# One kernel, four small moves in a hand-written order: a score copy ahead of a sign, and the first sorting for expert slots taken in one go

## The chip, the core and the metric

The kernel runs on one core of a Trainium2 chip. The metric is the device time of one execution in microseconds, as a median over runs. A core has five engines that run beside each other: TensorE (PE in the profile; its weight loads are PEld), VectorE (DVE), ScalarE (ACT), GpSimd (POOL) and SyncE (SP, which only issues transfers here). Each engine takes its own instructions strictly in the order in which the program gives them, and waits for the others through semaphores. So where an instruction stands in its engine's row is part of the program.

## What is computed

Attention with 8 batches, 8 heads, 576 positions and 64 features a head, in which every query keeps only its 32 largest scores; its output, as 4608 rows of 512, then goes through a layer of 8 experts of which each row takes one.

```python
scores = scale * np.matmul(q, k.transpose(0, 1, 3, 2))
kth = np.partition(scores, -32, axis=-1)[..., -32:-31]
scores = np.where(scores >= kth, scores, -1e9)
attn = np.exp(scores - scores.max(-1, keepdims=True))
attn = attn / (attn.sum(-1, keepdims=True) + 1e-09)
x = (attn @ v).transpose(0, 2, 1, 3).reshape(4608, 512)

logits = x @ w_gate
e_idx = np.argmax(logits, axis=1)
gate_w = softmax(logits)[np.arange(4608), e_idx]
eom = 1.0 / (1.0 + np.exp(-(x @ w_output_gate)))
for e in range(8):
    m = e_idx == e
    h = np.maximum(x[m] @ w1[e], 0.0)
    out[m] = gate_w[m, None] * eom[m, e, None] * (h @ w2[e])
```

## The kernel before

**Steps.** The queries are cut into 36 tiles of 128 rows, and each tile into four pairs of heads: 144 steps. Step i works on several pairs at once. On DVE it ranks the candidates of pair i (L317, L320), then for pair i-1 it does `spot` (L370, a small TENSOR_TENSOR), two window maxima (L359), the group maxima of pair i+1 (L309, 16 of them), then `pick` (L376, a small TENSOR_TENSOR), the threshold (L382) and the weighing of the exponentials by the threshold (L397). On ACT it makes two signs (L344) that POOL turns into the windows (L347, two TENSOR_TENSOR of 128x576), exponentials (L354), and copies out of PSUM. On PE it transposes the weighed exponentials of pair i-2 (L424), multiplies those of pairs i-4 and i-3 by the values in every second step (L456), and makes scores of a later pair (L282).

**Calm steps.** The first 40 steps (`LONE` = 40) are called calm in the code. In them the odd head of each pair is not weighed on DVE: DVE only negates its threshold (`less`, L385), ACT takes a sign with it (L404), POOL adds scores and sign (L407, a TENSOR_TENSOR of 128x576), and one step later ACT takes the exponential (L413). L404 and L407 are made by `veil`, for pair i-1 in step i; L413 by `unveil`, for pair i-2. Scores are made two pairs ahead there: PE's matmuls (L282) come after the last single transpose, which needs L413, and ACT's copy of them into SBUF (L290) is the first entry of a list `last` that runs after `veil`. In calm steps with an odd number PE also makes 24 (or 12) transposes that nobody reads (L977).

**Experts.** Every finished tile gets gate logits. After the tiles named in `SORTS` their rows are sorted (`group_route`, some 17 small DVE operations and two on ACT, with one matmul product between), and each tile's 128 list entries are scattered to DRAM by a GpSimd transfer (L589). `slot_picks` then chooses which experts get slots of 128 rows now, and how many; `queue_slots` puts them in `order`. In all 31 slots are made during the attention and 9 after it. The small operations wait in queues (`urgent`, `small`), of which `fill(n)` emits n at fixed places of a step; transfers wait in `slow`, from which `run_slow` emits as many as fit a budget (`DMAS` = 2.6, 2.0 in calm steps).

**A slot.** SP loads the slot's list of rows (L757), 2 MB of `w1` (L742) and 2 MB of `w2` (L749); GpSimd gathers its rows of x (L765); PE turns them (L775); then four pieces follow, one a step: two up (L786, 16 matmuls in the program, shown as 32 rows in the profile, each followed by a Relu on ACT, L794) and two down (L801). `ahead` fetches; `heavy_start` and `heavy_piece` set the pieces on PE's row. In the program before, the first slot is queued in step 38 and its first piece is in step 42, and from then on there is a piece in each step: 27 slots begin within the 144 steps and the four that drain the pipeline. A short stretch follows in which pieces already begun are finished, one with each call of `background`; there the last route, the table of the last slots and a check (`unsettled`, whose one matmul is L185) are made. The other 13 slots are worked after it in another form (L1107), with 48 matmuls of 512 columns each.

Of the kernel before, what the change touches and what calls it, by code (L numbers as in the profile page):

```python
# [23 lines left out]
P = 128  # L24


SORTS = ((4, 0), (7, 5), (11, 2), (13, 3), (16, 3), (19, 4), (23, 4), (27, 3), (30, 3), (32, 4))

USUAL = 9

# [2 lines left out]
DMAS = 2.6  # L33
# [5 lines left out]
def tile_topk_attention_moe(  # L39
# [39 lines left out]
    ids = dram.tile([NID, 4], I32, name="ids")  # L79
# [3 lines left out]
    for bp in range(NB // 2):  # L83
        for j in range(9):
# [4 lines left out]
            else:  # L89
                TT.append(((2 * bp + 1, j - 5),))  # L90
    sorts = [x for x in SORTS if x[0] < NTT]
    ENDS, EARLY = zip(*sorts) if sorts else ((), ())
    assert all(n <= E for n in EARLY) and E == 8
    ends = list(ENDS) + [NTT]
    GROUPS = [list(range(a, b)) for a, b in zip([0] + ends, ends)]
# [96 lines left out]
    def run(exact, stack):  # L192
# [15 lines left out]
        small = deque()  # L208
# [14 lines left out]
        def run_slow(budget, kinds):  # L223

            for x in [x for x in slow if x[2] in kinds]:
                if spent[0] + x[3] > budget:
                    return
                slow.remove(x)
                spent[0] += x[3]
                x[4]()  # L230

        def flush(what):
            for x in [x for x in slow if x[2] == what]:
                slow.remove(x)
                spent[0] += x[3]
                x[4]()

        def waiting(what):
            return any(x[2] == what for x in slow)

        def fill(n=1):
            for _ in range(n):
                if urgent:
                    urgent.popleft()()
                elif small and small[0]() is not False:
                    small.popleft()
# [64 lines left out]
        def rank(i, r):  # L311
            if exact:
                return
            vs, cs = VV[i]
            cs = [c.rearrange("p (g k) -> p g k", k=8)[:, :, :REACH[r]] for c in cs]
            for a in range(2):
                nc.vector.max(out=vs[:, a, 8 * r:8 * r + 8], in_=cs[a])  # L317
            if r < 2:
                for a in range(2):
                    nc.vector.match_replace(out=cs[a], in_to_replace=vs[:, a, 8 * r:8 * r + 8],  # L320
                                            in_values=cs[a], imm_value=LOW)
# [501 lines left out]
        NSTEP = NTT * NHP  # L823
# [3 lines left out]
        order = []  # L827
# [5 lines left out]
        def ahead(what, f, n, after=None, lag=0):  # L833

            while had[what] < min(len(order), cur[0] + n):
                s = had[what]
                if after and when.get((after, s), clock[0]) + lag > clock[0]:
                    return
                f(s, *order[s])
                when[what, s] = clock[0]  # L840
                had[what] += 1

        def queue_slots(g, n, rows):
            flush("x")
            assert rows_done[0] >= rows
            order.extend((g, k, rows) for k in range(n))
            known[0] = step[0] + (0 if had["id"] == cur[0] and not heavy else 1)
# [3 lines left out]
        def ids_known():  # L851

            ahead("id", fetch_id, len(order))
            assert had["id"] - cur[0] <= NLIST - 2
# [6 lines left out]
        def ahead_of_slot():  # L861

            clock[0] += 1
            fetch_ahead()
# [32 lines left out]
        def side_use():  # L897
            if uses:
                fill(len(urgent))
                uses.pop()()  # L900
# [22 lines left out]
            nc.tensor.transpose(awake[:, 0, :], ident, ident)  # L923
        scores(0)(((0, 1), (1, 2)))

        def route(g):
            small.extend(group_route(g, LGT[g]))
            if g < NGRP - 1 and EARLY[g]:
                small.extend(slot_picks(g))
                small.append(lambda: not waiting("ids"))  # L930
                small.append(lambda: queue_slots(g, EARLY[g], (GROUPS[g][-1] + 1) * P))
                small.append(lambda: step[0] >= known[0] and ids_known())
# [6 lines left out]
        for i in range(NSTEP + 4):  # L939
            t, hp = divmod(i, NHP)  # L940
            step[0] = i
            if i + 1 < NSTEP and (i + 1, 0) not in SC:
                scores(i + 1)()


            calm = i < LONE and not exact
            for r in range(3):
                if i < NSTEP:
                    rank(i, r)
                    if r == 0:  # L950
                        shift(i)
                if not calm:
                    fill(1)
            spent[0] = 0.0
            run_slow(SUMS, ("x",))
            spent[0] = 0.0
            if i < NSTEP:
                below(i)
            early, late, last = [], [], []
            mid, beside = None, None  # L960
            if calm and 2 <= i:
                first_copy = flip(i - 2, 0)
                mid = ps_t.tile([P, 4, P], F32, name="pst")
                f = side_start()
                beside = f(mid) if f else None
                first_copy()
            if 2 <= i < NSTEP + 2:
                unveil(i - 2)
            if calm:
                exps(i)  # L970
            if 4 <= i < NSTEP + 4 and i % 2 == 0:
                early.append(attend(i - 4))
            elif 2 <= i < LONE:

                idle = ps_m.tile([P, 4, P], F32, name="pm")
                for c in range(12 if beside else 24):
                    nc.tensor.transpose(idle[:, c % 4, :], ident, ident)  # L977
            if mid is not None:
                early.append(flip(i - 2, 1, beside, mid))
            elif 2 <= i < NSTEP + 2:  # L980
                early.append(flip(i - 2, 0))
                early.append(flip(i - 2, 1, side_start()))
            if calm and i + 2 < NSTEP:
                last.append(scores(i + 2))
            if i >= NSTEP + 2:
                extra = side_start()
                if extra:
                    early.append(extra(ps_t.tile([P, 4, P], F32, name="pst")))

            room = not uses  # L990
            ahead_of_slot()
            heavy_start()
            ev = heavy_piece()
            if ev:
                late.append(ev)
            if 2 <= i < NSTEP + 2:
                (last if calm else late).append(flip(i - 2, 2))
            ev = turn_ahead() if room or not heavy else None
            if ev:
                (last if calm else late).append(ev)  # L1000
            for f in early:
                f()
            if i < NSTEP and not calm:
                exps(i)
            for f in late:
                f()
            if 1 <= i <= NSTEP:
                spot(i - 1)
                window(i - 1, 0)
                window(i - 1, 1)  # L1010
            if i + 1 < NSTEP:
                gmax(i + 1, 0)
            if i + 1 < NSTEP:
                gmax(i + 1, 1)
            if 1 <= i <= NSTEP:
                pick(i - 1)
            if not calm:
                fill(1)
            if 1 <= i <= NSTEP:
                choose(i - 1)  # L1020
                fill(5 if calm else 1)
                weigh(i - 1)
            ahead("x", fetch_x, 2, "id", 1)
            run_slow(DMAS - 0.6 if calm else DMAS, ("ids", "out"))
            if 1 <= i <= NSTEP:
                veil(i - 1)
            for f in last:
                f()
            side_use()
            fill(3)  # L1030
            if i < NSTEP:
                if hp == 0 and t + 2 < NTT:
                    load_q(t + 2)
                if i == 0:
                    small.extend(([] if exact else setup()) + [clear_ids])
                jj = t % 9
                b2 = t // 9 * 2
                for j0, b in ((0, b2 + 1), (5, b2 + 2)):
                    n = (jj - j0) * NHP + hp
                    if b < NB:  # L1040
                        if n == 1:
                            load_k(b)
                        if n == 6:
                            load_v(b)
            if i >= 3 and (i - 3) % NHP == NHP - 1:
                tt = (i - 3) // NHP
                if tt == GROUPS[gi][0]:
                    LGT[gi] = st.tile([P, max(map(len, GROUPS)), 16], F32, name="lg", bufs=2)
                tile_rows(tt, gi, LGT[gi], tt - GROUPS[gi][0])
                if tt == GROUPS[gi][-1]:  # L1050
                    gi += 1
# [263 lines left out]
```

## Time and profile before

| | |
|---|---|
| median of 3 runs | 1270.94 us (1270.91 to 1271.02) |
| the profiled execution's own time | 1270.56 us |
| its span in the trace | 1268.8 us, so 1.76 us lie around it |
| mean granted TensorE clock | 0.984 |
| PE, DVE busy | 1178.6 and 1178.5 us |
| ACT, POOL busy | 1021.7 and 692.0 us |

How to read it: the trace gives every instruction a line of the code, a start, and what its engine waited for. A row of the timeline is start, duration, engine, line, operation, output and inputs, number merged; in brackets the idle time ahead of it and who ended it. A row of windows gives, for a stretch of the span, the busy time of PE, PEld, DVE, ACT and POOL with instruction counts, then the granted PE clock (1.00 is full speed), the share of the transfer engines and GB/s.

### The profile page before, as it was taken

To read this page: it belongs to the slowest core of one execution; us is meant where nothing else is said; L and a number is where in the kernel's file an instruction comes from. 1 tells how busy PE (TensorE), PEld (TensorE's weight loads), DVE (VectorE), ACT (ScalarE), POOL (GpSimd) and SP (SyncE) were. 2 spreads that over 40 slices of the span, in tenths; PEclk is the share of its full clock that TensorE was granted. 3 is DMA by queue.
4 is the path that set the end of the run, shared out by engine and by line. 5 is a ranking of instruction groups with operands and counts; after the bars stand their busy time and mean duration, and the time that the engine had idled before them with its cause. 6 is when DMAs were issued, how large, how long until landed. Compare 5 with 4: busy or idle time off the path is not lost.

```text
span 1268.8 us, 30920 instructions
## 1 busy us (share of the span) xinstructions
PE 1178.6 (93%) x9769; PEld 894.7 (71%) x9769; DVE 1178.5 (93%) x6045; ACT 1021.7 (81%) x1958; POOL 692.0 (55%) x1048
## 2 busy tenths in 40 slices
PE   6887778879999999999999999999999999899996
PEld 5665555557777777777777777777777777678885
DVE  7999999999999999999999999999999994689984
ACT  6999999987888778878888888878888884388883
POOL 6666676674467665664564475456556663232110
PEclk8999999988999999999999999999999999899998
DMA  5400210237446555656557556554444445899981
GB/s 138 78 18 18 72 56 18 56 118 245 167 165 204 174 203 179 215 192 222 183 197 228 189 184 204 182 202 167 167 167 167 167 165 213 317 376 396 391 310 60
DMA packets 109376, 227.39 MB, mean 179 GB/s; under 512 B 14855, under 2 KB 33543, under 8 KB 108177
## 3 DMA queue, kind: packets, MB, share of 16 engines
q1 hardware_dynamic: 99824, 205.67, 47.0%
q0 software_dynamic: 7552, 18.96, 4.2%
q8 instruction: 79, 1.29, 0.4%
q10 hardware_dynamic: 1824, 0.67, 0.3%
q14 instruction: 97, 0.79, 0.2%
HBM read 206.68 MB, written 20.69 MB: 179 GB/s over the span
## 4 chain that ended last, share of the span: by engine, by line
DVE 66%; PE 15%; issue 11%; ACT 5%; POOL 1%; DMA 1%; DVEq 0%; POOLq 0%; SPq 0%; ACTq 0%
DVE cand L309 20%; DVE v L359 12%; DVE ep L397 11%; DVE cand L320 7%; DVE v L317 6%; PE pm L786 4%; PE po L456 3%; DVE x L376 2%; PE ps L282 2%; DVE x L370 2%; DVE kth L382 2%; PE pst L424 1%; PE pm L801 1%; PE pm L1107 1%; ACT marks L344 1%
## 5 line engine op out<-in xcount | busy, mean ns | idle before, releaser
L347 POOL TENSOR_TENSOR w<-s,marks 128x576 f32<-128x576 f32 x288 | 363.3, 1283 | 202.6 <-ACT marks L344 183.1
L309 DVE MAX8 cand<-s 128x8 f32<-128x72 f32 x2304 | 321.9, 216 | 12.9 <-ACT s L290 12.8
L424 PE MATMUL pst<-ident,ep 128*128 128x128 f32 x1296 | 206.3, 283 | 46.0 <-ACT ep L413 32.5
L344 ACT ACTIVATE marks<-s,v 128x576 int8<-128x576 f32 x288 | 220.6, 770 | 23.8 <-DVE v L317 21.7
L432 ACT ACTIVATE pT<-pst 128x512 f32<-128x512 f32 (+1 forms) x432 | 197.7, 483 | 51.8 <-PE pst L424 50.4
L424 PEld LDWEIGHTS pst<-ident,ep 128*128 128x128 f32 x1296 | 145.5, 141 | 132.9 <-issue 48.7
L786 PE MATMUL pm<-xs,w1t 128*128 128x128 f32 x1792 | 212.3, 277 | 0.0
L786 PEld LDWEIGHTS pm<-xs,w1t 128*128 128x128 f32 x1792 | 206.7, 194 | 0.2 <-issue 0.2
L359 DVE MAX8 v<-w 128x8 f32<-128x576 f32 x288 | 203.3, 746 | 0.0
L397 DVE SCALAR_TENSOR_TENSOR ep<-s,kth,ep 128x576 f32<-128x576 f32 x248 | 194.8, 817 | 8.6 <-DVE kth L382 0.5
L290 ACT ACTIVATE s<-ps 128x1152 f32<-128x1152 f32 (+1 forms) x145 | 162.2, 1120 | 50.3 <-PE ps L282 49.9
L801 PE MATMUL pm<-w2t,ht 128*128 128x512 f32 x432 | 194.4, 593 | 0.0
L456 PE MATMUL po<-pT,v 128*64 128x128 f32 (+3 forms) x3200 | 186.4, 268 | 0.0
L282 PE MATMUL ps<-kst,qst 64*128 64x288 f32 (+1 forms) x1280 | 179.5, 428 | 5.2 <-ACT s L290 5.2
L354 ACT ACTIVATE ep<-s,v 128x576 f32<-128x576 f32 x248 | 181.0, 779 | 3.1 <-POOL v L333 3.1
L456 PEld LDWEIGHTS po<-pT,v 128*64 128x64 f32 (+1 forms) x3200 | 159.0, 137 | 33.7 <-issue 31.9
L812 POOL DMA_INDIRECT out_dram<-y,idt x40 | 45.6, 1140 | 160.5 <-ACT y L808 147.8
L801 PEld LDWEIGHTS pm<-w2t,ht 128*128 128x128 f32 x432 | 78.0, 191 | 77.5 <-issue 77.5
L317 DVE MAX8 v<-cand 128x8 f32<-128x24 f32 (+2 forms) x864 | 132.2, 194 | 0.0
L282 PEld LDWEIGHTS ps<-kst,qst 64*128 64x128 f32 (+1 forms) x1280 | 97.0, 176 | 44.2 <-issue 17.5
L320 DVE MATCH_REPLACE8 cand<-v,cand 128x24 f32<-128x24 f32 (+1 forms) x576 | 97.5, 178 | 0.0
L333 POOL TENSOR_SCALAR v<-v 128x2 f32<-128x2 f32 x144 | 32.8, 227 | 113.8 <-DVE v L317 112.7
(185 smaller groups left out, 1689.6 us busy)
## 6 DMA issues: line engine op xcount, KB each, us to landing
w1t<-in_w_dram SPq DMA_DIRECT2D x40, 2048.0 KB
w2t<-in_w_dram SPq DMA_DIRECT2D x40, 2048.0 KB
v<-in_va_dram SPq DMA_DIRECT2D x8, 1152.0 KB
x_rows<-xu SPq DMA_DIRECT2D x36, 256.0 KB
qst<-in_qa_dram SPq DMA_DIRECT2D x70, 128.0 KB
kst<-in_ka_dram SPq DMA_DIRECT2D x14, 576.0 KB
ids<-far SPq DMA_DIRECT2D x1, 678.0 KB
xg<-x_rows,idt POOLq DMA_INDIRECT x40, 6.4
```

The costliest lines, as they stand in the source:

```text
L282: nc.tensor.matmul(ps[qs, a, n, :288], Q[t][rows, hp, qs], K[b][rows, hp, cols], start=True, stop=True)
L309: nc.vector.max(out=c[:, 8 * g:8 * g + 8], in_=SC[i, a][:, g * GW:(g + 1) * GW])
L317: nc.vector.max(out=vs[:, a, 8 * r:8 * r + 8], in_=cs[a])
L344: nc.scalar.activation(m.bitcast(I8).rearrange("p (s b) -> p s b", b=2)[:, :, 1], s, AF.Sign, bias=vs[:, a, PIVOT - 1:PIVOT], scale=-(1.0 ...
L347: nc.gpsimd.tensor_tensor(w, s, m, op=ALU.add)
L359: nc.vector.max(out=VV[i][0][:, a, 24:32], in_=SW[i][0][a])
L397: nc.vector.scalar_tensor_tensor(e, SC.pop((i, a)), kth_col(i, a), e, op0=ALU.is_ge, op1=ALU.mult, accum_out=SM[t][:, 2 * hp + a:2 * hp + ...
L424: nc.tensor.transpose(ps[:, c - c0, :], pt[:, c * P:(c + 1) * P], ident)
L432: nc.scalar.activation(x, ps[:, :n, :], AF.Copy)
L456: nc.tensor.matmul(po[a * 64:(a + 1) * 64, k, qs], lhs, rhs, start=half and not k and not m, stop=(c == 3 and k == 1 and m == len(TT[t]) - 1))
L786: nc.tensor.matmul(ph[:, f - f0, :], w[:, c, f * P:(f + 1) * P], XS[s][:, c, :], start=(c == 0), stop=(c == NC - 1))
L801: nc.tensor.matmul(PY[s], HT[s][:, f, :], w[:, f, :], start=(f == 0), stop=(f == NF - 1))
```

## The change

Four edits. In calm steps the copy of the scores (L290), first in the list `last`, is put ahead of `veil`'s sign of the odd head (L404). The first sorting covers five tiles instead of four; it has no slots (`(5, 0)`), so the second sorting, the first with slots, covers tiles 5 and 6 instead of 4 to 6. From the second route on until its slots are queued a flag `hurry` holds: `fill(60)` takes all small operations that can go, at two places of the step, with the open use of PE's side product (`side_use`) ahead of the first; the budget of `run_slow` is 3.4. And the first slots are queued, listed and get their first `w1` and `w2` fetched in the same step (`first_fetches`).

```diff
-SORTS = ((4, 0), (7, 5), (11, 2), (13, 3), (16, 3), (19, 4), (23, 4), (27, 3), (30, 3), (32, 4))
+SORTS = ((5, 0), (7, 5), (11, 2), (13, 3), (16, 3), (19, 4), (23, 4), (27, 3), (30, 3), (32, 4))
...
+        hurry = [False]
+
+        def first_fetches():
+            hurry[0] = False
+            ids_known()
+            ahead("w1", fetch_w1, 1)
+            ahead("w2", fetch_w2, 1)
+
         def route(g):
             small.extend(group_route(g, LGT[g]))
             if g < NGRP - 1 and EARLY[g]:
                 small.extend(slot_picks(g))
+                if not order:
+                    hurry[0] = True
+                    small.append(lambda: not waiting("ids"))
+                    small.append(lambda: queue_slots(g, EARLY[g], (GROUPS[g][-1] + 1) * P))
+                    small.append(first_fetches)
+                    return
...
             if 1 <= i <= NSTEP:
                 choose(i - 1)
-                fill(5 if calm else 1)
+                if hurry[0]:
+                    side_use()
+                fill(60 if hurry[0] else 5 if calm else 1)
                 weigh(i - 1)
             ahead("x", fetch_x, 2, "id", 1)
-            run_slow(DMAS - 0.6 if calm else DMAS, ("ids", "out"))
+            run_slow(DMAS + 0.8 if hurry[0] else DMAS - 0.6 if calm else DMAS, ("ids", "out"))
+            if last and calm and i + 2 < NSTEP:
+                last.pop(0)()
             if 1 <= i <= NSTEP:
                 veil(i - 1)
             for f in last:
                 f()
             side_use()
             fill(3)
+            if hurry[0]:
+                fill(60)
```

In the order of instructions the first edit shows on ACT in every calm step. This is the place in step 2, rows with a minus from the program before, with a plus from the changed one; `marks_81` is the sign of the odd head, `s` the copied scores, `pT` copies of transposes, `marks_79` the first sign of the next step:

```order
 L354 ACTIVATE ep<-s,v_286 128x576
 L432 ACTIVATE pT_385<-pst 128x128
-L404 ACTIVATE marks_81<-s,less 128x576
-L290 ACTIVATE s<-ps 128x1152
+L290 ACTIVATE s<-ps 128x1152
+L404 ACTIVATE marks_81<-s,less 128x576
 L432 ACTIVATE pT_397<-pst 128x512
 L344 ACTIVATE marks_79,n<-s,v_403 128x576
```

Only L404 and L290 have changed places; all else on ACT stays as it was in these steps.

The other edits move the experts' pieces. This is PE's row in step 37, a calm step, in the program before: transposes, the idle ones (L977), one transpose more, the scores, and the transposes of the end of this step and the start of the next.

```order
L424 MATMUL pst<-ident,ep 128x128 x8
L977 MATMUL pm<-ident 128x128 x24
L424 MATMUL pst<-ident,ep 128x128
L282 MATMUL ps<-kst,qst 128x288 x4
L424 MATMUL pst<-ident,ep 128x128 x8
```

And the same step in the changed program, where L991 is the line of the idle transposes:

```order
L424 MATMUL pst<-ident,ep 128x128 x4
L991 MATMUL pm<-ident 128x128 x24
L424 MATMUL pst<-ident,ep 128x128
L282 MATMUL ps<-kst,qst 128x288 x4
L786 MATMUL pm<-xs,w1t 128x128 x16
L424 MATMUL pst<-ident,ep 128x128 x4
L775 MATMUL pst<-ident,xg_124 128x128 x4
L424 MATMUL pst<-ident,ep 128x128 x4
```

The first piece of the first slot (L786) has come into step 37, behind the scores, and with it the turn of the second slot's rows (L775); the idle transposes stay. In the changed program pieces stand in steps 37 to 56 and from 59 on; 28 slots begin ahead of the tail instead of 27, and 12 are left for the last form instead of 13.

At the end of the attention this stands on PE around L185, the matmul of the check, before (L558 is the last product of the route; L1086 turns rows for the last form):

```order
L558 MATMUL pst<-oh_17003,ones_b 128x8
L801 MATMUL pm<-w2t,ht 128x512 x4
L185 MATMUL po<-lo,ones 1x2
L786 MATMUL pm<-xs,w1t 128x128 x16
L1086 MATMUL pm<-ident,xg_124 128x128 x4
```

And in the changed program:

```order
L558 MATMUL pst<-oh_17038,ones_b 128x8
L801 MATMUL pm<-w2t,ht 128x512 x4
L775 MATMUL pst<-ident,xg_124 128x128 x4
L801 MATMUL pm<-w2t,ht 128x512 x4
L185 MATMUL po<-lo,ones 1x2
L786 MATMUL pm<-xs,w1t 128x128 x16
```

One down piece more stands between the route's product and the check's matmul.

## The prediction

> **What bounds the kernel now.** First the page's head and busy times, then windows by stage.
>
> ```profile
> span 1268.8 us, 30920 instructions
> ...
> PE 1178.6 (93%) x9769; PEld 894.7 (71%) x9769; DVE 1178.5 (93%) x6045; ACT 1021.7 (81%) x1958; POOL 692.0 (55%) x1048
> ```
>
> ```profile
> 80.00:120.00 40.00, 32.89 (x336) 24.25 (x337) 39.45 (x239) 38.48 (x83) 26.97 (x35) 1.00 0.05 15
> 231.00:234.00 3.00, 1.27 (x11) 0.83 (x10) 2.96 (x24) 2.47 (x6) 1.44 (x3) 1.00 0.02 5
> 234.00:237.00 3.00, 3.00 (x32) 2.65 (x34) 3.00 (x17) 3.00 (x9) 2.66 (x4) 0.58 0.37 120
> 250.00:300.00 50.00, 38.88 (x330) 30.66 (x326) 48.97 (x278) 41.08 (x87) 33.95 (x46) 0.86 0.51 187
> 500.00:600.00 100.00, 99.27 (x838) 74.58 (x837) 97.86 (x555) 81.29 (x168) 59.87 (x97) 1.00 0.57 195
> ```
>
> PE and DVE tie over the span, but not by stage. In calm steps (80 to 120 us) DVE is busy 39.45 of 40 and PE 32.89: DVE sets the pace, and PE is idle in places, waiting. Once pieces of slots run (500 to 600) PE is at 99.27 and DVE at 97.86, so both set it. The third stage is the tail, 12 to 13 slots in the last form, where the chain that ended last is PE's own work:
>
> ```profile
> 1157.95 9.58 issue
> ...
> 1206.94 9.57 issue
> ```
>
> Every slot there repeats the same long entry; between these two lie four slots, (1206.94 - 1157.95) / 4 = 12.25 us each.
>
> **The tail: -12.2.** The changed order begins 28 slots ahead of the tail instead of 27, so one period of 12.25 us goes. One piece more stands ahead of the check's matmul instead. These are PE's rows there:
>
> ```profile
> 1084.08 3.68 PE L801 MATMUL pm<-w2t,ht 128*128 128x512 f32 x8
> 1093.28 0.19 PE L185 MATMUL po<-lo,ones 128*1 128x2 f32 x2 [5.52 <-DVE lo L183]
> 1093.40 6.03 PE L786 MATMUL pm<-xs,w1t 128*128 128x128 f32 x32
> ```
>
> The last down piece ends at 1087.8, then PE idles 5.52 us for DVE's table and check, and starts again slowly. A second down piece of 3.68 us fits in that hole, so it costs nothing; if DVE came earlier there, it would cost its 3.68. The end gives between -8.6 (piece paid) and -14.5 (the slow restart, 6.03 for what takes 3.74 below, goes too). I take -12.2.
>
> **The swap on ACT: +14.** The four operations around it, in one calm step from `spot` to `spot`:
>
> ```profile
> 206.74 0.30 DVE L370 TENSOR_TENSOR x<-left,n 128x16 f32<-128x16 f32 x1
> 206.98 0.78 ACT L344 ACTIVATE marks<-s,v 128x576 int8<-128x576 f32 x1
> 207.92 2.51 POOL L347 TENSOR_TENSOR w<-s,marks 128x576 f32<-128x576 f32 x2 [0.15 <-ACT marks L344]
> 208.97 0.77 ACT L413 ACTIVATE ep<-w,v 128x576 f32<-128x576 f32 x1
> ...
> 210.15 1.24 PE L282 MATMUL ps<-kst,qst 64*128 64x288 f32 x8
> 210.45 0.15 DVE L376 TENSOR_TENSOR x<-x,v 128x16 f32<-128x16 f32 x1
> ...
> 211.08 0.78 ACT L404 ACTIVATE marks<-s,less 128x576 int8<-128x576 f32 x1
> 211.77 1.11 ACT L290 ACTIVATE s<-ps 128x1152 f32<-128x1152 f32 x1
> 212.01 1.28 POOL L407 TENSOR_TENSOR w<-s,marks 128x576 f32<-128x576 f32 x1 [1.44 <-ACT marks L404]
> 212.78 0.59 ACT L432 ACTIVATE pT<-pst 128x512 f32<-128x512 f32 x1
> 213.02 0.30 DVE L370 TENSOR_TENSOR x<-left,n 128x16 f32<-128x16 f32 x1
> ```
>
> The sign L404 is ready at 211.08, but the scores on PE end only at 210.15 + 1.24 = 211.39. With the copy first, it starts at about 211.42; the copy holds ACT for 212.78 - 211.77 = 1.01, so the sign starts at 212.43, 1.35 later than now. POOL's L407 follows the sign by 212.01 - 211.08 = 0.93: it moves from 212.01-213.29 to 213.36-214.64. Nobody wants the copy earlier: DVE uses those scores a step later.
>
> That L407 is later would not matter by its result, which is read a step later. It matters by what it runs beside. `spot` at 213.02 takes 0.30 and ends 0.03 after L407; look at it and at `pick` elsewhere:
>
> ```profile
> L370 DVE TENSOR_TENSOR x<-left,n x144: 152/158/2031, 15.4 to 1057.4; 128x16 f32<-128x16 f32 x144
> ```
>
> ```profile
> 277.20 1.29 POOL L407 TENSOR_TENSOR w<-s,marks 128x576 f32<-128x576 f32 x1
> 277.30 1.23 DVE L370 TENSOR_TENSOR x<-left,n 128x16 f32<-128x16 f32 x1
> ...
> 303.34 2.52 POOL L347 TENSOR_TENSOR w<-s,marks 128x576 f32<-128x576 f32 x2 [3.80 <-ACT marks L344]
> 304.71 1.19 DVE L376 TENSOR_TENSOR x<-x,v 128x16 f32<-128x16 f32 x1
> ```
>
> The median `spot` takes 158 ns. The one issued at 277.30, in the middle of L407, ends at 278.53, just as L407 does at 278.49; the `pick` issued in L347's second half ends 0.04 after it. So a two-input DVE operation stands still until POOL's two-input operation is over. Counted from a `spot` at 206.74, L407 now covers 5.27 to 6.55 of a step of 6.28, and the next `spot` is held by 0.14. After the swap it covers 6.62 to 7.90. A step shorter than 6.62 slips past: its `spot` goes free, but then L407, the small shift behind it and L347 come 0.66 later on POOL, so that `pick`, which now comes in just as L347 ends (207.92 + 2.51 = 210.43 against 210.45), waits some 0.67. A longer step has its `spot` inside L407, held until 7.93. Both lengthen the step; and a long step makes the next wait shorter.
>
> ```profile
> 81.67 2.15 DVE cand L309 x16
> 107.71 2.15 DVE cand L309 x16
> ...
> 259.55 2.15 DVE cand L309 x16
> ...
> 310.55 2.15 DVE cand L309 x16
> ```
>
> Four calm steps take (107.71 - 81.67) = 26.04, or 6.51 each. Carrying the two waits through such a group of four with the offsets above, I get about 7.0 a step: +0.5. By the simple balance, a step and the one before it sum to 6.51 plus 7.93 less the 0.3 of wait already there, half of which is 7.07.
>
> ```profile
> L407 POOL TENSOR_TENSOR w<-s,marks x40: 1267/1280/1414, 20.8 to 283.7; 128x576 f32<-128x576 f32 x40
> ```
>
> L407 runs 40 times. Leaving out the first two, the five last, which the pieces rule (below), and some five in which a sorting makes the step so long that L407 is over by the next `spot`, 28 are left: 28 x 0.5 = **+14**. Bounds: -4 (28 x 0.14, if every `spot` escapes and no `pick` is caught) and +30 (28 x 1.07, each `spot` held as at 277.30, above its median). I stay by the balance, since a held step frees the next one, and put +22, 0.8 a step, as the most that I expect.
>
> **First pieces in calm steps: +7.** Five more pieces come in steps 37 to 41, two fewer in 57 and 58.
>
> ```profile
> 295.55 3.74 PE L786 MATMUL pm<-xs,w1t 128*128 128x128 f32 x32
> ...
> 299.32 0.60 ACT L794 ACTIVATE ht<-pm 128x512 f32<-128x512 f32 x1 [1.59 <-PE pm L786]
> ```
>
> ```profile
> 279.78 2.23 DVE L309 MAX8 cand<-s 128x8 f32<-128x72 f32 x16
> ```
>
> In a calm step ACT's Relu (L794) stands ahead of the copy, the sign, a transposes' copy and then the next step's signs. From L344 to L413 are 1.99 us, to the scores' end 2.42, to the Relu 3.77; then 0.48 for the Relu (as the pT copy of its shape, 212.78 until the next L344 at 213.26), 1.01 copy, 0.69 sign, 0.48 pT: a loop of 10.8 us through ACT and PE.
>
> ```profile
> 213.26 0.77 ACT L344 ACTIVATE marks<-s,v 128x576 int8<-128x576 f32 x1
> ```
>
> Step 37 adds 0.5 for the turn's copy; step 39 has a down piece, no Relu, and about 9. That is 31 for steps 37 to 39, where the group maxima at 259.55 (step 37) and 279.78 (step 40) lie 20.2 apart. So +11; but the pieces of 40 and 41 go into PE's idle time (11.1 of 50 us between 250 and 300), and steps 42 and 43, in which the first pieces of the program before begin, lose that start: the four steps from 279.78 to 310.55 take 30.8 there. I give back 4 of these, and take **+7**. Bounds: the five pieces are 18 us of PE; filling all 11.1 idle us they cost +3 with the slow stretch regained, and nothing given back makes +12. In 57 and 58 DVE still sets the pace, 97.86 of 100: -0.3.
>
> **Sorting in one go: 0; five tiles: 0.** DVE gets the same operations, at steps 24 to 28 and 32 to 33 instead of 20 to 24 and 32 to 36.
>
> ```profile
> 255.79 1.12 PE L424 MATMUL pst<-ident,ep 128*128 128x128 f32 x4 [2.95 <-DVE tl L511]
> 256.70 5.27 PE L977 MATMUL pm<-ident 128*128 128x128 f32 x24
> ```
>
> PE's stall behind them (2.95, then a slow stretch) goes from step 36 and comes back in 33, where `weigh` now waits behind some twenty operations; DVE was busy all the while, so it neither gains nor loses. DVE may wait a little for ACT's two small exponentials, which stand behind the swapped sign: -2 to +2. SP's lists and first weights are four steps earlier on a queue with little to do (0.05 of the transfer engines at 80 to 120), three steps ahead of the first piece.
>
> **Sum.** -12.2 + 14 + 7 - 0.3 = +8.5 on the profiled execution's 1270.56 us, 1.76 of it around the span; the median shown is 0.38 above it. So 1279.4 by the median, said as **1279.5**.
>
> **Rivals.** *A, the swap is free* (`spot` escapes, `pick` is not caught, or PE's scores come earlier than at 211.39): -12.2 + 7 - 0.3, 1265.5, faster. For it: at 6.28 the `spot` does slip past; against it, `pick` has 0.02 us of room. It decides once the swap costs under 5 in all, 0.18 a step. *B, it costs half*: 1272.5, no change. *C, PE turns cold in the loop of steps 37 to 39*, where it idles some 2 us of each 11. The rows 231 to 237 show it: busy 1.27 of 3 us, then a granted clock of 0.58, and at 1093.40 a piece takes 6.03. Three pieces by 2.4 and the scores and transposes among them make +10: 1290, slower. The Trainium skill (TensorE: Matmul & The Clock Gate, Part 1: The HAM clock gate) says that the clock falls after an idle window of about 3.4 us; by that the loop stays warm and C does not come. The trace differs at 231 to 237, where no idle stretch was that long. *D, the change doesn't do what it says*: the gathers or weights come so late that step 37's piece waits, on top of the forecast, up to a step, 1287.
>
> **Chances.** Forecast (1274 to 1287) 0.57; A 0.19; B 0.09; C and D 0.15. A measurement tells about 0.2%, 2.5 us, from no change. Faster by more is A alone, 0.19; within it B, 0.09; slower the rest, 0.72. The range from 1263 to 1291 takes in A, B, the swap's +22 with the rest as forecast (1287.5) and C, and leaves out the ends in which both unknown costs lie at one extreme (from 1257 to 1303).
>
> **What would show it.** In the changed profile `spot`'s (L370) or `pick`'s rows in calm steps last 0.5 us or more, ending 0.03 after L407 or L347, and four calm steps take 28 us; if they still take 26, the swap's term is wrong. Steps 37 to 39 take about 31 us with ACT waiting for PE ahead of L794. PE's wait at L185 shrinks to 2 us, and the tail has 12 periods of 12.25. A PE clock under 1 in steps 37 to 39 is C.

## The result, and the profile after

| | before | after |
|---|---|---|
| median | 1270.93 us (4 runs, 1270.37 to 1271.02) | 1285.28 us (4 runs, 1285.22 to 1287.79) |
| profiled execution: own time, span | 1270.56, 1268.8 us | 1287.79, 1286.0 us |

The changed kernel is slower: ratio 1.0119, 95% interval 1.0101 to 1.0136. The profiled execution of after lies 2.5 us above its median, so its stages together show that much too much. The head of its page:

```profile
span 1286.0 us, 30908 instructions
...
PE 1186.3 (92%) x9781; PEld 896.8 (70%) x9781; DVE 1183.9 (92%) x6038; ACT 1015.6 (79%) x1952; POOL 687.9 (53%) x1048
```

The totals of the engines have hardly moved. So the span is cut into stages at the starts of steps 0, 32, 44 and 143 (the first rank maximum, L317, of a step). The windows of before, and then of after, by these bounds; the second number of a row is its length:

```profile
10.43:218.22 207.79, 161.91 (x1591) 121.64 (x1591) 205.07 (x1250) 192.67 (x409) 144.85 (x200) 0.98 0.21 52
218.22:307.69 89.47, 72.17 (x632) 56.52 (x631) 87.13 (x502) 76.82 (x163) 57.05 (x74) 0.90 0.44 148
307.69:1051.05 743.36, 737.38 (x6429) 548.26 (x6427) 726.76 (x4096) 602.66 (x1227) 437.59 (x699) 1.00 0.54 185
1051.05:1268.80 217.75, 199.72 (x1082) 162.17 (x1080) 157.39 (x185) 146.78 (x158) 48.66 (x60) 0.97 0.79 295
```

```profile
11.23:233.38 222.15, 165.40 (x1592) 122.92 (x1592) 219.44 (x1250) 194.32 (x409) 144.08 (x200) 0.96 0.20 47
233.38:343.79 110.41, 90.53 (x710) 68.58 (x710) 94.50 (x504) 78.85 (x167) 60.38 (x77) 0.89 0.54 182
343.79:1080.95 737.16, 731.42 (x6386) 543.96 (x6385) 721.34 (x4098) 602.05 (x1225) 433.83 (x697) 1.00 0.54 183
1080.95:1286.00 205.05, 190.81 (x1057) 154.72 (x1055) 146.44 (x178) 137.53 (x150) 45.73 (x59) 0.99 0.80 291
```

Steps 0 to 31 take 14.4 us more, and DVE's busy time grows by as much (14.4), though its work is the same: it stands still inside instructions. Steps 32 to 43 take 20.9 more, and there DVE's busy time grows by only 7.4. Steps 44 to 142 take 6.2 less, the rest 12.7 less. With 0.8 more ahead of step 0 that is 17.2, the difference of the spans.

The calm stage by the chain that ended last, four steps from one `cand` to the other, (101.41 - 73.25) / 4 = 7.04 us each, where it was 6.51:

```profile
73.25 2.15 DVE cand L309 x16
...
101.41 2.15 DVE cand L309 x16
```

One step of it in the timeline: the copy ahead of the sign, a wait for PE in front of the copy, and POOL's and DVE's two-input rows beside each other:

```profile
80.01 2.51 POOL L347 TENSOR_TENSOR w<-s,marks 128x576 f32<-128x576 f32 x2
81.45 1.10 DVE L376 TENSOR_TENSOR x<-x,v 128x16 f32<-128x16 f32 x1
82.75 1.13 ACT L290 ACTIVATE s<-ps 128x1152 f32<-128x1152 f32 x1 [0.56 <-PE ps L282]
83.78 0.77 ACT L404 ACTIVATE marks<-s,less 128x576 int8<-128x576 f32 x1
84.70 1.28 POOL L407 TENSOR_TENSOR w<-s,marks 128x576 f32<-128x576 f32 x1 [2.05 <-ACT marks L404]
84.96 1.05 DVE L370 TENSOR_TENSOR x<-left,n 128x16 f32<-128x16 f32 x1
```

`pick` (L376) ends at 82.55, 0.03 after L347 (82.52), and `spot` (L370) at 86.01, 0.03 after L407 (85.98): both waits that the prediction named, with the rows that it named. The wait of the copy, 0.56, it had in its working but not as a cost.

The first pieces, in the timeline of ACT and PE:

```profile
280.97 1.24 PE L282 MATMUL ps<-kst,qst 64*128 64x288 f32 x8
282.14 3.84 PE L786 MATMUL pm<-xs,w1t 128*128 128x128 f32 x32
286.01 0.60 ACT L794 ACTIVATE ht<-pm 128x512 f32<-128x512 f32 x1 [4.53 <-PE pm L786]
286.51 1.12 ACT L290 ACTIVATE s<-ps 128x1152 f32<-128x1152 f32 x1
289.13 0.80 ACT L344 ACTIVATE marks<-s,v 128x576 int8<-128x576 f32 x1
300.02 0.79 ACT L344 ACTIVATE marks<-s,v 128x576 int8<-128x576 f32 x1
309.80 0.77 ACT L344 ACTIVATE marks<-s,v 128x576 int8<-128x576 f32 x1
```

The scores are done at 282.21 and are copied at 286.51, since ACT stands in front of the Relu. From 289.13 the next steps of the ring take 10.9 and 9.8 us. What DVE waits for most in that stretch, in after (277 to 345 us) and, below it, in before (255 to 308), as total, times and longest (in after it also waits 3.0 us once for another copy, L479):

```profile
DVE cand L309 <- ACT s L290: 11.2, 5, 4.2
```

```profile
DVE cand L309 <- ACT s L290: 0.6, 1, 0.6
```

And the tail: PE's wait at L185, and two of the entries that repeat at every slot, five periods apart (61.32 / 5 = 12.26 us):

```profile
1123.43 0.19 PE L185 MATMUL po<-lo,ones 128*1 128x2 f32 x2 [1.50 <-DVE lo L183]
```

```profile
1177.09 9.60 issue
...
1238.41 9.60 issue
```

### The profile page after: what moved, and what is told of

It reads as the page before. It is cut to its first block, busy times and chain, and to the rows that moved or that the text cites. A ratio compares the mean times of both kernels' runs of the same rounds, so it can differ in the third digit from the quotient of the medians.

```text
span 1286.0 us, 30908 instructions
## 1 busy us (share of the span) xinstructions
PE 1186.3 (92%) x9781; PEld 896.8 (70%) x9781; DVE 1183.9 (92%) x6038; ACT 1015.6 (79%) x1952; POOL 687.9 (53%) x1048
## 4 chain that ended last, share of the span: by engine, by line
PE 56%; DVE 30%; issue 9%; ACT 2%; POOL 1%; DMA 1%; POOLq 0%; DVEq 0%; SPq 0%; ACTq 0%
PE pm L786 15%; PE pm L801 12%; DVE cand L309 9%; PE po L456 9%; PE ps L282 8%; PE pst L424 8%; DVE v L359 5%; DVE ep L397 4%; DVE cand L320 3%; DVE v L317 3%; DVE x L370 2%; DVE x L376 1%; DMA w1t<-in_w_dram 1%; PE pst L476 1%; POOL xg L765 1%
## 5 line engine op out<-in xcount | busy, mean ns | idle before, releaser
L347 POOL TENSOR_TENSOR w<-s,marks 128x576 f32<-128x576 f32 x288 | 363.3, 1283 | 171.7 <-ACT marks L344 155.7
L344 ACT ACTIVATE marks<-s,v 128x576 int8<-128x576 f32 x288 | 220.8, 770 | 35.2 <-DVE v L317 31.5
L290 ACT ACTIVATE s<-ps 128x1152 f32<-128x1152 f32 (+1 forms) x145 | 162.7, 1123 | 71.2 <-PE ps L282 71.2
L786 PE MATMUL pm<-xs,w1t 128*128 128x128 f32 x1856 | 218.7, 276 | 0.1
L786 PEld LDWEIGHTS pm<-xs,w1t 128*128 128x128 f32 x1856 | 213.4, 193 | 1.1 <-issue 0.8
L801 PE MATMUL pm<-w2t,ht 128*128 128x512 f32 x448 | 202.3, 594 | 0.0
L456 PE MATMUL po<-pT,v 128*64 128x128 f32 (+3 forms) x3200 | 188.6, 269 | 0.0
L282 PE MATMUL ps<-kst,qst 64*128 64x288 f32 (+1 forms) x1280 | 182.1, 433 | 5.2 <-ACT s L290 5.2
L456 PEld LDWEIGHTS po<-pT,v 128*64 128x64 f32 (+1 forms) x3200 | 160.9, 138 | 34.2 <-issue 32.5
L801 PEld LDWEIGHTS pm<-w2t,ht 128*128 128x128 f32 x448 | 80.8, 190 | 80.9 <-issue 80.9
L317 DVE MAX8 v<-cand 128x8 f32<-128x24 f32 (+2 forms) x864 | 131.9, 193 | 0.0
L407 POOL TENSOR_TENSOR w<-s,marks 128x576 f32<-128x576 f32 x40 | 51.2, 1279 | 86.8 <-ACT marks L404 86.8
## 6 DMA issues: line engine op xcount, KB each, us to landing
kst<-in_ka_dram SPq DMA_DIRECT2D x14, 576.0 KB, 14.2
```

The costliest lines, as they stand in the source:

```text
L282: nc.tensor.matmul(ps[qs, a, n, :288], Q[t][rows, hp, qs], K[b][rows, hp, cols], start=True, stop=True)
L344: nc.scalar.activation(m.bitcast(I8).rearrange("p (s b) -> p s b", b=2)[:, :, 1], s, AF.Sign, bias=vs[:, a, PIVOT - 1:PIVOT], scale=-(1.0 ...
L347: nc.gpsimd.tensor_tensor(w, s, m, op=ALU.add)
L456: nc.tensor.matmul(po[a * 64:(a + 1) * 64, k, qs], lhs, rhs, start=half and not k and not m, stop=(c == 3 and k == 1 and m == len(TT[t]) - 1))
L786: nc.tensor.matmul(ph[:, f - f0, :], w[:, c, f * P:(f + 1) * P], XS[s][:, c, :], start=(c == 0), stop=(c == NC - 1))
L801: nc.tensor.matmul(PY[s], HT[s][:, f, :], w[:, f, :], start=(f == 0), stop=(f == NF - 1))
```

## The experiments

Times are medians, with the ratio to the kernel before on the same chip (1270.16 to 1270.71 us there) and its interval. Stages are cut as above.

| kernel | us | ratio (95%) | steps 0-31 | 32-43 | 44-142 | rest |
|---|---|---|---|---|---|---|
| before | 1270.93 | | 207.8 | 89.5 | 743.4 | 217.7 |
| after | 1285.28 | 1.0119 (1.0101-1.0136) | 222.2 | 110.4 | 737.2 | 205.1 |
| e1 after, no swap | 1269.99 | 1.0001 (0.9991-1.0011) | 207.0 | 110.2 | 737.2 | 203.8 |
| e2 before, swap | 1286.15 | 1.0125 (1.0108-1.0142) | 221.4 | 91.6 | 743.0 | 218.1 |
| e3 e2, spot late | 1338.96 | 1.0526 (1.0506-1.0546) | 221.2 | 93.3 | 795.7 | 217.2 |
| e4 after, from step 39 | 1281.57 | 1.0095 (1.0077-1.0112) | 221.2 | 103.2 | 739.5 | 204.4 |
| f1 e2, no L407 | 1365.36 | 1.0750 (1.0732-1.0768) | 214.6 | 89.1 | 743.1 | 306.6 |
| f2 before, no L407 | 1351.21 | 1.0638 (1.0621-1.0656) | 202.7 | 85.6 | 743.4 | 307.0 |
| f3 e1, Relu later | 1268.90 | 0.9991 (0.9980-1.0003) | 207.2 | 107.2 | 737.2 | 207.0 |
| f4 e1, from step 39 | 1265.44 | 0.9966 (0.9951-0.9980) | 207.4 | 100.4 | 739.4 | 207.3 |
| g1 f1, scores first | 1365.56 | 1.0743 (1.0726-1.0759) | 214.1 | 90.1 | 743.3 | 305.9 |
| g2 f4, scores ahead | 1267.53 | 0.9972 (0.9960-0.9984) | 208.1 | 103.8 | 739.5 | 207.3 |
| g3 f3, no idle transposes | 1262.84 | 0.9935 (0.9920-0.9950) | 207.6 | 103.5 | 737.2 | 203.0 |
| g4 g3, scores ahead | 1266.48 | 0.9968 (0.9956-0.9980) | 207.4 | 107.2 | 737.3 | 202.5 |

### One part alone: the swap (e1, e2)

e1 takes the swap out of the changed kernel, e2 puts it alone into the kernel before:

```diff
-            if last and calm and i + 2 < NSTEP:
-                last.pop(0)()
```

> The changed kernel with the copy of the scores behind the odd head's sign again (the order of before); all else as changed. Theory 'shared wait' (the later L407 of POOL holds DVE's spot and pick): steps 0 to 31 fall back from about 7.0 to 6.5 us each, 14 us in all, and the time to about 1270. Rival 'pieces' (the loss is the five pieces and the sorting in one go, and the swap is harmless): no more than 2 us faster than the changed kernel, 1283 to 1285.

> The kernel before with the swap alone. Theory 'shared wait': calm steps of about 7.0 us, 14 to 17 us slower than before, 1285 to 1288. Rival 'pieces': within 2 us of before, 1269 to 1273.

Measured: 1269.99 and 1286.15. The swap costs 15.3 us in the changed kernel and 15.7 in the old one, 13.6 of it (e2) in steps 0 to 31. All other edits together are worth nothing measurable: in e1 the 13.9 us less of the rest and 6.2 less of steps 44 to 142 are eaten by the 20.7 that steps 32 to 43 take more.

### Where the swap's cost comes from (e3, f1, f2, g1)

e3 moves `spot` on DVE behind the two window maxima, out of reach of L407:

```diff
-                spot(i - 1)
                 window(i - 1, 0)
                 window(i - 1, 1)
+                spot(i - 1)
```

> As e2, but spot (L370) stands behind the two window maxima on DVE instead of ahead of them; the same operations, one place moved. Theory 'shared wait': spot comes some 1.4 us later, when L407 is nearly over, and waits 0.1 us instead of 0.8; pick is still held by L347 in some steps. A calm step takes about 6.75 us, 7 to 9 us less than e2 in all. Rival 'ACT chain' (the swap costs because the odd head's sign and exponential come later on ACT and PE waits for them, whatever POOL holds): the same time as e2 within 2 us.

Measured: 1338.96 us, 53 more than e2. Steps 0 to 31 did not change (221.2 against 221.4), so moving `spot` saved nothing. The 53 come from the later steps, where `spot` had not been held and now falls into L347. All 144 of its rows in e3, min, median and max in ns, and a pair of rows of step 100:

```profile
L370 DVE TENSOR_TENSOR x<-left,n x144: 155/986/2614, 17.2 to 1129.3; 128x16 f32<-128x16 f32 x144
```

```profile
777.51 2.52 POOL L347 TENSOR_TENSOR w<-s,marks 128x576 f32<-128x576 f32 x2 [1.79 <-ACT marks L344]
777.84 0.99 DVE L370 TENSOR_TENSOR x<-left,n 128x16 f32<-128x16 f32 x1
```

`spot` is held until 778.83, when the first of the two L347 is over (777.51 + 1.28, as one alone lasts). The median was 158 ns and is 986. The wait for POOL is real and dear. In calm steps it was only moved: between 60 and 200 us `spot` takes 520 ns in the mean (670 in e2) and `pick` 411 (315), now held by L347 for the most part. So e3 does not decide between the two theories.

f1 and f2 leave out the addition L407 (the odd head's sum reads the scores unchanged; f1 with the swap, f2 without). Their outputs send rows to other experts, and the tail is 89 us longer in both, so the totals that were written down do not hold; they are compared only with each other and in steps 0 to 31.

```diff
-                w = wk.tile([P, S], F32, name="w", bufs=3)
-                nc.gpsimd.tensor_tensor(w, SC.pop((i, 1)), marks[2], op=ALU.add)
-                VE[i] = w
+                VE[i] = SC.pop((i, 1))
```

> The kernel before with the swap on ACT alone, and with GpSimd's addition behind the sign (L407) left out: the odd head's sum of exponentials reads the scores themselves. If the swap costs because L407 stands beside DVE's spot and pick, nothing is left of its 15.7 us: within 3 us of the kernel before without the same addition, about 1262 to 1271 us, with spot near 0.16 to 0.3 us in calm steps. If it costs because ACT does the sign 1.35 us later and its own order is what the step waits for, it stays 12 to 16 us above the other, about 1277 to 1283.

> The kernel before with GpSimd's addition behind the odd head's sign (L407) left out, in its old order on ACT: the control for the run with the swap. By both theories 1263 to 1270 us: the 0.14 us by which spot is held in a calm step of 6.28 goes, at most 0.2 us in each of 28 calm steps, which is up to 6 us.

Measured: f1 is 14.2 us above f2, and 11.9 in steps 0 to 31 (214.6 against 202.7), where e2 was 13.6 above before. So most of the cost is there without L407 too. The groups of ACT's copy, its signs and `pick`, between 60 and 200 us, in f1 and below it in f2 (busy us, mean ns of one, idle before them):

```profile
L290 ACT ACTIVATE s<-ps 128x1152 f32<-128x1152 f32 x21 | 23.8, 1131 | 11.3 <-PE ps L282 11.3
L344 ACT ACTIVATE marks<-s,v 128x576 int8<-128x576 f32 x41 | 31.4, 774 | 0.0
L376 DVE TENSOR_TENSOR x<-x,v 128x16 f32<-128x16 f32 x21 | 10.3, 492 | 0.0
```

```profile
L290 ACT ACTIVATE s<-ps 128x1152 f32<-128x1152 f32 x21 | 23.5, 1121 | 0.3 <-PE ps L282 0.3
L344 ACT ACTIVATE marks<-s,v 128x576 int8<-128x576 f32 x44 | 33.8, 773 | 2.3 <-DVE v L317 2.3
L376 DVE TENSOR_TENSOR x<-x,v 128x16 f32<-128x16 f32 x21 | 3.9, 186 | 0.0
```

`spot` takes 157 ns in both. What f1 has and f2 has not is ACT's wait for PE's scores, 11.3 us in 21 steps, 0.54 each, and then a later `pick`. In the old order the sign filled that gap. In f1 ACT has no slack ahead of the next step's signs (L344), where it waits 2.3 us for DVE in f2. So, counted from the step's start, it begins these signs 0.3 to 0.55 us later in 19 of the steps 8 to 31, L347 follows, and `pick` is held until L347 is over:

```profile
77.88 2.51 POOL L347 TENSOR_TENSOR w<-s,marks 128x576 f32<-128x576 f32 x2 [1.95 <-ACT marks L344]
79.72 0.71 DVE L376 TENSOR_TENSOR x<-x,v 128x16 f32<-128x16 f32 x1
```

The 0.31 us of `pick` are most of what a calm step is longer: steps 9 to 12 take 26.96 us in f1 and 25.45 in f2, 0.38 each.

With L407 in place the rows say something else. The signs, `spot` and `pick` in the same stretch, in e2 and below it in before:

```profile
L344 ACT ACTIVATE marks<-s,v 128x576 int8<-128x576 f32 x40 | 30.7, 771 | 4.1 <-DVE v L317 4.1
L370 DVE TENSOR_TENSOR x<-left,n 128x16 f32<-128x16 f32 x20 | 13.4, 670 | 0.0
L376 DVE TENSOR_TENSOR x<-x,v 128x16 f32<-128x16 f32 x19 | 6.0, 315 | 0.0
```

```profile
L344 ACT ACTIVATE marks<-s,v 128x576 int8<-128x576 f32 x42 | 32.2, 772 | 3.3 <-DVE v L317 3.0 <-POOL v L333 0.3
L370 DVE TENSOR_TENSOR x<-left,n 128x16 f32<-128x16 f32 x21 | 6.0, 283 | 0.0
L376 DVE TENSOR_TENSOR x<-x,v 128x16 f32<-128x16 f32 x21 | 3.4, 161 | 0.0
```

Here `spot` and `pick` together take 0.54 us a step more, mostly `spot` behind L407, and steps 9 to 12 are 0.56 longer each (28.29 us against 26.05): by the trace the held rows are the whole lengthening. ACT is not late at L344; it waits there for DVE, 4.1 us in e2. So f1 does not show that L407 is harmless. It shows that a second limit, ACT's queue, lies close behind it and costs 0.38 us a step when L407 is away.

g1 takes that wait away in f1: PE gets the scores ahead of the transpose that waits for ACT.

```diff
-            if calm and i + 2 < NSTEP:
-                last.append(scores(i + 2))
...
+            if calm and i + 2 < NSTEP:
+                last.append(scores(i + 2))
             if mid is not None:
                 early.append(flip(i - 2, 1, beside, mid))
```

> The kernel before with the swap and without GpSimd's addition L407, as the earlier run, and with PE's eight matmuls of the scores moved ahead of the one transpose that waits for ACT's exponential (L413) in calm steps; ACT's order is that of the swap. That earlier run took 214.6 us for steps 0 to 31, its control without the swap 202.7. If what is left of the swap's cost is ACT standing idle until PE's scores are there, with its work of about 6.2 us in every calm step of 6.3 to 6.5, the scores are now there in time: 203 to 207 us for steps 0 to 31, 1351 to 1356 us in all. If the late sign itself costs it, 212 to 216 us and 1361 to 1366.

Measured: 214.1 us for steps 0 to 31, in the range expected if the late sign itself costs the time. By steps it says more. Steps 9 to 12 of g1:

```profile
67.26:73.39 6.13, 4.72 (x42) 3.45 (x42) 6.06 (x41) 5.86 (x14) 3.44 (x5) 1.00 0.00 0
73.39:79.51 6.12, 4.38 (x49) 3.28 (x49) 6.05 (x40) 6.12 (x14) 2.87 (x4) 1.00 0.31 90
79.51:85.92 6.41, 6.01 (x39) 4.72 (x39) 6.31 (x43) 4.73 (x12) 2.87 (x4) 0.73 0.00 0
85.92:94.78 8.86, 6.82 (x74) 5.39 (x73) 7.61 (x42) 7.99 (x18) 3.98 (x5) 1.00 0.01 3
```

Steps 9 to 11 take 18.66 us; f2 takes 18.72 and f1 19.95 for the same three, so there the swap's cost is gone. Step 12 takes 8.86, against 6.73 in f2, because PE's new order makes ACT wait for transposes (9.7 us in 8 waits between 60 and 165 us). That the wait for the scores carries what is left of the cost without L407 is supported by three steps of four; the long fourth step also gives ACT time to catch up, so it is not settled cleanly. With L407 in place nobody took that wait away.

### Where the first pieces' cost comes from (e4, f3, f4, g2, g3, g4)

e4 and f4 hold the first piece until step 39, with the swap (as in after) and without it:

```diff
-            if heavy or when.get(("turn", s), clock[0]) >= clock[0]:
+            if heavy or step[0] < 39 or when.get(("turn", s), clock[0]) >= clock[0]:
                 return
```

> The changed kernel, but no piece starts ahead of step 39 (one calm step with a piece instead of three; the same 28 slots ahead of the tail, no gap at steps 57 and 58). Theory 'loop' (each calm step with a piece takes 10 to 11 us through ACT and PE): two steps less of it, 7 to 9 us given back, less the 2 us that the gap at 57 and 58 saved, so 1278 to 1281. Rival (pieces cost PE time alone, wherever they stand): 1284 to 1287.

> The changed kernel without the swap and with the first piece not before step 39 instead of 37; the tail still begins 28 slots behind. With the swap in, the same shift gave 3.7 us. If the two costs stand apart, 1265 to 1267.5; if the swap's longer calm steps were part of what the shift gave back, 1269 to 1271.

Measured: 1281.57, 3.7 less than after and just above what the ring would give, and 1265.44, 4.6 less than e1, as expected. The two costs stand apart. Steps 32 to 43 shrink by 7.2 and 9.8, and steps 44 to 63 give back 2.3.

f3 gives the Relu of a calm step's piece to ACT a step later, behind the next two signs and the exponentials; g3 also drops the idle transposes in calm steps that have a piece:

```diff
+            while held:
+                held.pop()()
...
-            elif 2 <= i < LONE:
+            elif 2 <= i < LONE and not heavy:
...
             ev = heavy_piece()
             if ev:
-                late.append(ev)
+                (held if calm else late).append(ev)
```

> The changed kernel without the swap; in calm steps the Relu of a piece (L794) is given to ACT one step later, behind the next step's two signs and its exponential, and no longer ahead of the scores' copy. If the first pieces cost what they cost because ACT and PE wait for each other in a ring through that Relu, steps 37 to 39 (32.8 us without the swap) shrink to 25 to 28 and steps 40 to 42 (31.2) by 2 to 5: 1257 to 1264 us. If PE is simply full there with the pieces, ACT's order does not matter: 1267 to 1271.

> As the run with the Relu behind the next signs, and without the 12 idle transposes (L991) in calm steps that have a piece: there, PE waited 3.1 us in step 39 because these transposes write a bank that the late Relu had still to read, and that step and the next took 23.3 us. If that wait is what ate the gain of steps 37 and 38, 1263 to 1266 us; if the scores behind the pieces in steps 40 to 42 set the end anyway, 1267 to 1270.

Measured: f3 1268.90, in the range expected if PE is full. Its steps 38 and 39 are shorter, though (6.3 and 8.2 us, in e1 10.4 and 12.6), and step 40 has 15.1 (9.8 in e1). There PE waits for the late Relu with the idle transposes, which write a bank that the Relu reads; in g3 the same place waits 1.96 and for the exponential. The rows of f3 and of g3:

```profile
283.26 0.98 PE L994 MATMUL pm<-ident 128*128 128x128 f32 x7 [3.11 <-ACT ht L794]
```

```profile
283.21 0.33 PE L424 MATMUL pst<-ident,ep 128*128 128x128 f32 x1 [1.96 <-ACT ep L413]
```

g3 took 1262.84, 7.2 less than e1, and steps 32 to 43 took 103.5 instead of 110.2. The gain lies in steps 37 to 39 (20.9 us, 29.5 in e1); steps 40 to 43 gained nothing (40.7, 39.5 in e1). So a large part of what the pieces cost in steps 37 to 39 was the order on ACT, not their work on PE. Two things go along with it. PE's clock stayed at 1.00 from 258 to 327 us in g3, where e1 has 0.72 from 270 to 276 and from 282 to 288. And no run leaves out the idle transposes alone; by e1's trace they held nothing up there, since the transpose behind them starts at 285.98, just as the exponential that it needs is done (285.05 + 0.79 = 285.84). With every other edit of the change but the swap in it, g3 beats both kernels: 0.9935 of before, interval 0.9920 to 0.9950.

g2 and g4 put the scores' matmuls of steps 40 to 43 in front of the step's piece on PE; ACT's order stays:

```diff
-            if calm and i + 2 < NSTEP:
+            if i < 44 and i + 2 < NSTEP and not exact:
                 last.append(scores(i + 2))
```

> The changed kernel without the swap, first piece not before step 39, and in steps 40 to 43 the scores of two steps ahead are given to PE in front of the step's piece, no longer at the start of the next step behind it; ACT's order stays. If steps 40 to 43 are long (39.4 us in the run without this edit) because DVE's group maxima wait for scores that stand behind a piece on PE, they take 31 to 35 and the kernel 1257 to 1262 us. If PE is full there with the pieces whatever their order, 1264 to 1267.

> The run before this and the scores ahead of the pieces in steps 40 to 43 together, pieces from step 37 as in the change. If both the ring through the Relu and the scores behind the pieces cost what they seem to, steps 37 to 43 take 52 to 58 us (69.0 in the changed kernel without the swap) and the kernel 1254 to 1261 us. If PE is full there, 62 or more and 1263 to 1268.

Measured: 1267.53 and 1266.48, 2.1 and 3.6 more than without the edit, and steps 32 to 43 3.4 and 3.7 longer. Both theories' reason was wrong. PE was not full (36.95 of 42.77 us in steps 40 to 43 of g2), yet early scores did not help:

```profile
299.56 2.29 PE L282 MATMUL ps<-kst,qst 64*128 64x288 f32 x8
301.78 4.83 PE L801 MATMUL pm<-w2t,ht 128*128 128x512 f32 x8
306.45 0.60 PE L424 MATMUL pst<-ident,ep 128*128 128x128 f32 x4
307.09 0.60 ACT L432 ACTIVATE pT<-pst 128x512 f32<-128x512 f32 x1 [5.82 <-PE pst L424]
308.06 1.14 ACT L290 ACTIVATE s<-ps 128x1152 f32<-128x1152 f32 x1
```

The scores were done at 301.85, but their copy stands on ACT behind copies that need what PE makes after the piece, and that piece only came later. By this trace the queue that holds DVE up there is ACT's; no run made these four steps shorter.

## Why the prediction was right, and where not

The median, 1285.28 us, lies in the range (1263 to 1291) and on the side that had 0.72; the point, 1279.5, was 5.8 too low. By its own steps:

- **Tail, -12.2: right.** 12.7 less, periods of 12.26. PE's wait at L185 shrank from 5.52 to 1.50 (2 was said), so the second down piece cost nothing. Between kernels with the same tail the rest varies from 202.5 to 207.3 us. Of the 4.4 us between f4 and g3 one wait of PE for a copy on ACT (`hs`) makes 2.7 (4.2 against 1.5); what makes it longer was not tried.
- **Swap on ACT, +14: right in size, place and rows, with a second limit overlooked.** 15.3 and 15.7 by e1 and e2, 14.4 in steps 0 to 31. The rows came as described: sign and L407 late, `spot` and `pick` ending 0.03 after POOL, steps of 7.04 for the said 7.0, and in e2 the held rows make 0.54 of the 0.56 us by which a step is longer. But the step that fails in part is that the cost comes by POOL's later L407 alone: without L407 11.9 of 13.6 us stay in steps 0 to 31 (f1 against f2), there through ACT, which waits 0.54 us a step for scores and so brings L347 late to `pick`. The working had both numbers, scores at 211.39 and ACT at 38.48 of 40, and priced only what came behind. That the two limits cost nearly the same was not foreseen. How much of L407's lateness is due to ACT's wait, and whether DVE would wait for ACT elsewhere if `pick` were free, is open.
- **First pieces, +7: the ring right, the give-back wrong.** Steps 37 to 43 take 68.0 instead of 51.0, +17.0, beyond the bound of +12. The ring itself was 32.0 (277.78 to 309.80) for the said 31. The 4 us to be given back in steps 40 to 43 did not come: these four take 39.5 instead of 31.8, +7.7. DVE waits in the stretch for copies (11.2 us against 0.6) that stand behind a piece's evictions on ACT; scores given earlier to PE did not help (g2), and what would is open, since g3 got its time back in steps 37 to 39 alone. Rival C, a cold PE, came late and in part: the granted clock is 1.00 from 277 to 300 us, but 0.66 from 300 to 305, in step 39, and again from 320 to 325. The working's "three pieces by 2.4" should read 2.3 (6.03 - 3.74).
- **Sorting in one go, 0 (-2 to +2): at the edge of its range.** In e1, without the swap, steps 32 to 36 take 2.7 more and steps 0 to 31 take 0.8 less, +1.9 together. In after steps 32 to 36 take 4.0 more. PE's stall came back in step 33 as said, with a slow clock behind it: the matmuls L456 that take 2.55 elsewhere take 4.73.

```profile
254.19 1.09 PE L424 MATMUL pst<-ident,ep 128*128 128x128 f32 x4 [2.98 <-DVE v L317]
255.21 4.73 PE L456 MATMUL po<-pT,v 64*64 64x128 f32 x40
```

- **Steps 57 and 58, -0.3: too small.** Steps 44 to 63 take 3.6 less and 64 to 142 another 2.6. e4 and f4 have as many pieces there as before (50 down, 49 up) and still take 3.9 less, so the two pieces are worth 2.3 and most of it has another cause. PE's busy time falls by 6.0 in these steps together and DVE's by 5.4, so the windows do not say which of the two sets the pace; it stays open.

The terms as e1 measures them: +20.7 in steps 32 to 43, -6.2 behind them, -13.9 in the rest, -0.8 in steps 0 to 31 and -0.7 ahead of them make -0.9, and the swap's +15.3 makes +14.4, the difference of the two medians. The forecast's two large misses, 10 too little for the first pieces and 6 too little gain in steps 44 to 142, cancelled in part; that the point came so near is luck to that extent. The end of 1303 that the working names for both costs at their upper bounds should be 1300.4 (1270.94 - 12.2 - 0.3 + 30 + 12); nothing else rests on it.

## What to carry to other kernels

When an instruction is moved on a queue that is nearly full, price the hole that it used to fill on that queue as well as the waits that it makes farther on, on other engines: here either alone would have cost most of it. A run without the blamed instruction shows whether another limit stands close behind; that the cost stays does not clear the instruction, so read in both kernels which rows became longer. And, in steps like these, an eviction that waits for a long matmul belongs behind everything in that queue which the next step needs.

## What the runs showed that was not expected

`spot`, 158 ns by itself, took 986 ns at the median when it was placed beside POOL's L347 in every step, and 53 us of the kernel's time (e3). An instruction of 128x16 elements so cost 0.53 us in each of the 99 steps from 44 on ((795.7 - 743.0) / 99) by its place alone. The Trainium skill (SBUF — State Buffer, Summary: rules for kernel authors) says that when a DVE operation has two inputs in SBUF while a GpSimd operation reads SBUF, the second one to be issued blocks until the first is finished; the rows of e3 and the 0.03 us by which the held rows end behind POOL's agree.

The idle transposes that fill a hole on PE make a wait of their own where the bank that they write is still to be read: 3.11 us in f3.
